# One pool for the eight PSUM banks, score halves placed alone, and two more transposes through the DMA crossbar, with new instruction lists

## The chip, the core and the metric

The kernel runs on one core of one Trainium2 chip. The metric is the device time of one execution in microseconds (us); the profile takes one execution apart by engine: PE (TensorE matmul) and PEld (its weight loads), ACT (ScalarE), DVE (VectorE), POOL (GpSimd) and SP (SyncE). POOL and SP issue nearly all DMAs here.

## What is computed

Two stages in a row, cut from the reference. The first is attention with ALiBi bias in a sliding window of 128, over 8 batches, 8 heads, 576 positions and head dimension 64:

```python
scores = scale * np.matmul(q, k.transpose(0, 1, 3, 2))
mask = (rel >= 0) & (rel < window)
scores = np.where(mask, scores + bias[None], -1000000000.0)
attn = np.exp(scores - max); attn = attn / (attn.sum + 1e-09)
x = np.matmul(attn, v)            # then (batch, seq, 8 * 64 = 512)
```

The second is an RWKV channel mix over x with the row before it (x_prev):

```python
xk = mu_k * x + (1 - mu_k) * x_prev
xr = mu_r * x + (1 - mu_r) * x_prev
k = np.maximum(xk @ w_k, 0.0)     # 512 -> 1024
v = k * k @ w_v                   # 1024 -> 512
out = 1 / (1 + np.exp(-(xr @ w_r))) * v
```

Inputs and output are fp32, and the matmuls run in bf16.

## The kernel before

**Attention.** A batch b is worked in four groups g of two heads. q and k come in position-major and are turned so that head dimension lies on the partitions: on PE for batches 0 to 3 (L1126, L1123, qk_quad at L1078, qk_some at L837), by DMA transposes from SP for batches 4 to 7 (flip, L535). The last 64 positions of a batch, its tail, are a load of their own; they are turned by PE for batches 0 to 3 (tails at L939, tails_full at L912) and by a DMA transpose for 4 to 7 (tail_flip, L628; the range XTT). `scores` (L726) multiplies q by k for two halves of the window, HALF0 and HALF1; each half fills two PSUM banks (one per head) and only HALF1 reads the tail. ACT takes the exponential (L740) and DVE multiplies by the mask with the bias in it (L753). `attend` (L781) multiplies by v, whose column of ones gives the row sum, into two PSUM banks; DVE takes the reciprocal (L787) and scales (L793) into xu. xu is turned back to feature-major xt: for batches 1 to 5 two groups at a time on PE (out_some, L837, with two copies on ACT, L696), for 6 and 7 by a DMA transpose from SP (out_flip, L902; the range XO). DVE makes the difference with the shifted rows (L880) and xk and xr (L887).

**Channel mix.** `channel_mix` works on pairs P of batches, in stretches of 256, 384 or 512 rows. For each of eight slices fo: four matmuls of x with w_k into one PSUM bank (L983), ReLU on ACT (L990), square on DVE or ACT (L964, L962). For each 128 rows: four matmuls with w_r into one bank (L1001) and tanh on ACT (L1008); eight matmuls with w_v into one bank, in two halves of four (L1017); DVE joins both into ot (L1022); SP stores it (L1047).

**Order.** Every operation is a `Node` of a `Plan`. `ORDER` at the top holds three lists of node numbers, written out by hand for PE, ACT and DVE: each of these engines runs its nodes in that order and no other. POOL and SP follow priorities, FAB stands for the DMA engines. `Plan.run` walks through planned times with costs per node, hands out buffers and PSUM banks (`Hold`, `take`, `pick`: the lowest free number), and emits instructions by planned start. Semaphore waits between engines are put in after that, from the order in which instructions that touch a tile were emitted. 90 small matmuls (L687) fill PE's gaps in the first 17 us.

**PSUM.** 2 KB per partition and bank, eight banks. They are split into `duo`, two tiles of two banks each (class p2: score halves and attend), and `uno`, four tiles of one bank each (class p1: everything else). A node that computes both halves of a score takes both duo tiles at once.

```python
duo = [pst.tile([128, 2, 512], FP32, name=f"duo{i}") for i in range(2)]
uno = [pst.tile([128, 512], FP32, name=f"uno{i}") for i in range(4)]
def one(h):
    return uno[h.idx if h.cls == "p1" else N1 + h.idx]
def two(h):
    return duo[h.idx]
```

`SS` names the batches whose two score halves are nodes of their own (none before), and `OH` those that use out_some.

Of the kernel before, what the change touches and what calls it, by code (L numbers as in the profile page):

```python
# [9 lines left out]
FP32 = mybir.dt.float32  # L10
# [28 lines left out]
""".split()],  # L39
    "ACT": [int(x) for x in """  # L40
# [11 lines left out]
""".split()],  # L52
    "DVE": [int(x) for x in """
# [187 lines left out]
def kernel(  # L241
# [14 lines left out]
    B, H, S, D = q.shape  # L256
# [10 lines left out]
    W = D + 1  # L267
# [5 lines left out]
    NQ, NA, NX, NV, NC = 4, 4, 4, 2, 2  # L273
    XB = range(4, B)
    XO = range(6, B)
# [22 lines left out]
    SS = ()  # L298
    OH = range(1, 6)
# [15 lines left out]
    XTT = range(4, B)  # L315
# [53 lines left out]
    duo = [pst.tile([128, 2, 512], FP32, name=f"duo{i}") for i in range(2)]  # L369
    uno = [pst.tile([128, 512], FP32, name=f"uno{i}") for i in range(4)]  # L370
    N1 = 4
    PT = "p1"

    def one(h):
        return uno[h.idx if h.cls == "p1" else N1 + h.idx]

    def two(h):
        return duo[h.idx]

    plan = Plan(dict(qx=2, p2=2, p1=N1, pt=4 - N1, qk=NQ, at=NA, xu=NX, vs=NV, cb=NC, ts=2, tt=2, xt=2, dl=2, dl0=4,  # L380
                     xk=2, rl=3, kk=3, rs=4, ot=NO),
                {}, WAIT)
# [14 lines left out]
    def op(e, dur, deps, prio, emit, need=(), free=()):  # L397
        return plan.add(e, dur, LAT.get(e, 0.2) if isinstance(e, str) else LAT[e[0]] if len(e) == 1 else 0.22,
                        deps, prio, emit, need, free)
# [274 lines left out]
    h_mu = Hold("p1")  # L674
# [9 lines left out]
    h_wm = Hold("p1")  # L684
# [13 lines left out]
    def scores(b, g, parts, bias, hq, ha, deps, prio, need, free):  # L698

        todo, dur = [], 0.0  # L700
        for (pieces, m0, tt) in parts:
            a0 = BASE[pieces[0][0]] + pieces[0][1] - 128 * pieces[0][0]
            w = sum(n for _, _, n in pieces)
            todo.append((pieces, m0, tt, a0, w, Hold("p2")))
            dur += sum(max(n / 2400 + .0025, .03) for _, _, n in pieces)
            dur += 0.01 + (2 * mm(w) if bias else 0)
# [24 lines left out]
        s = op(PE, (0.12 if bias else 0.02) + dur, deps, prio + (2,), emit, list(need) + [x[5] for x in todo], free)  # L731
# [27 lines left out]
    def attend(b, g, t0, t1, ha, deps, prio):  # L759
# [3 lines left out]
        hp, hx = Hold("p1" if 2 * nt * W <= 512 else "p2"), Hold("xu")  # L763
# [5 lines left out]
        def a5():  # L769
            if hp.cls == "p1":  # L770
                return one(hp)[:, 0:2 * nt * W].rearrange("p (h t c) -> p h t c", h=2, c=W)
            return two(hp)[:, :, 0:nt * W].rearrange("p h (t c) -> p h t c", c=W)
# [36 lines left out]
    def out_t(b, g, t0, t1, hx, deps, prio, hk, ht, late=None):  # L809
# [3 lines left out]
        hp = Hold(PT if b else "p1")  # L813
# [15 lines left out]
    def halves(n, block):  # L829

        hp = [Hold("p1"), Hold("p1")]

        def emit(e):
            for i in range(n):
                src, c = block(i)
                for r in range(2):
                    nc.tensor.transpose(  # L837
                        one(hp[r]).bitcast(BF16)[:, c:c + 64], src[64 * r:64 * r + 64],
                        ident[64 * r:64 * r + 64, 64 * r:64 * r + 64])

        return hp, emit
# [65 lines left out]
    def tails_full(b, prio, htt, hs):  # L907
        hp = Hold("p1")
# [16 lines left out]
    def tails(b, prio):  # L925
# [8 lines left out]
        hp = Hold("p1")  # L934
# [33 lines left out]
    def channel_mix(P, c0, c1, first, xks, xrs, order):  # L968
# [9 lines left out]
        for fo in range(NFO):  # L978
            hp, hr = Hold("p1"), Hold("rl")
# [16 lines left out]
        for i, c in enumerate(range(c0 // 128, c1 // 128)):  # L996
            hp, hs = Hold("p1"), Hold("rs")
# [12 lines left out]
            hv, ho = Hold("p1"), Hold("ot")  # L1010
# [16 lines left out]
            for a, b in ((0, FIN), (FIN, 512)) if final else ((0, 512),):  # L1027
                if a:
                    hv = Hold("p1")
# [40 lines left out]
    def qk_quad(b, g, nr, buf, deps, prio, c0, hq, take, free):  # L1070

        hp = [Hold("p1"), Hold("p1")]
# [25 lines left out]
    for part in range(2):  # L1098
# [3 lines left out]
        for g in range(G):  # L1102
# [13 lines left out]
            hp = Hold("p1") if part == 0 else None  # L1116
# [51 lines left out]
    def mask_pe(j):  # L1168
        hp = Hold("p2")
# [55 lines left out]
    def qk_full(b, g, prio):  # L1225
        hp, hq = Hold(PT), Hold("qk")
# [101 lines left out]
```

## Time and profile before

| what | value |
|---|---|
| time, median of 3 runs (lowest to highest) | 229.33 us (228.99 to 229.42) |
| the profiled execution: its time, its span | 228.84 us, 227.1 us |
| PE busy | 221.8 us, 98% of the span |
| DVE busy | 188.8 us, 83% |
| ACT busy | 155.0 us, 68% |
| POOL busy | 92.0 us, 41% |
| share of PE in the chain that ended last | 92% |

The span runs from the first to the last instruction that the profiler saw; the execution's own time is 1.7 us more. Busy time of PE counts each matmul with the time its result takes to come out, so neighbours overlap. The chain that ended last is followed back from the last instruction to what released it; the windows view gives busy time by stretch, the groups view the mean duration of one instruction of each kind.

### The profile page before, as it was taken

What the parts mean: (1) busy time and instruction counts of PE and PEld (TensorE: products, weight loads), DVE (VectorE), ACT (ScalarE), POOL (GpSimd) and SP (SyncE); (2) the same over time, 40 slices, a digit from 0 to 9 for tenths busy, and PEclk for the clock granted to TensorE, in tenths of its full rate; (3) what the DMA queues carried; (4) which work ended last, traced back from release to release, by engine and by line L of the source; (5) the groups of instructions that cost most, each with busy time, mean ns of one, the idle gap of its engine ahead of it and who ended that gap; (6) DMA issues with size and microseconds to landing.
All of it is one profiled execution on the core that took longest, in us unless ns stands there. A gap on an engine that the chain in (4) does not pass through costs nothing.

```text
span 227.1 us, 6442 instructions
## 1 busy us (share of the span) xinstructions
PE 221.8 (98%) x2587; PEld 133.2 (59%) x2587; DVE 188.8 (83%) x423; ACT 155.0 (68%) x279; POOL 92.0 (41%) x118
## 2 busy tenths in 40 slices
PE   8899999999999999999999999999999999999994
PEld 8576766755666755556666554546765455446552
DVE  6786999899879998899978996999899988963433
ACT  0678999999989984975868358768567564047511
POOL 8856726599962964385208750240000000000000
PEclk9999999999999999999999999999999999999999
DMA  6999999999999999999999999999150415430124
GB/s 165 179 185 200 197 196 175 199 180 151 196 156 165 137 130 180 168 182 147 211 180 158 120 185 231 177 136 222 30 135 3 123 46 52 131 136 3 49 92 139
DMA packets 129981, 33.19 MB, mean 146 GB/s; under 512 B 116632, under 2 KB 126112, under 8 KB 129952
## 3 DMA queue, kind: packets, MB, share of 16 engines
q0 software_dynamic: 95728, 16.26, 97.5%
q1 hardware_dynamic: 32480, 15.94, 34.1%
q10 hardware_dynamic: 1744, 0.59, 1.1%
q8 instruction: 20, 0.33, 0.6%
q14 instruction: 9, 0.07, 0.1%
HBM read 33.56 MB, written 9.44 MB: 189 GB/s over the span
## 4 chain that ended last, share of the span: by engine, by line
PE 92%; ACT 3%; DMA 2%; SPq 1%; issue 0%; DVE 0%; DVEq 0%; ACTq 0%
PE uno L983 28%; PE uno L1017 28%; PE uno L1001 13%; PE duo L726 7%; PE duo L781 7%; DMA qx<-in_q_dram 2%; PE uno L837 2%; PE uno L1078 2%; ACT at L740 1%; PE duo L713 1%; ACT qk L696 1%; PE uno L781 1%; SPq L550 1%; PE uno L687 1%; PE uno L820 1%; PE uno L939 0%
## 5 line engine op out<-in xcount | busy, mean ns | idle before, releaser
L983 PE MATMUL uno<-xk,wk_sb 128*128 128x256 bf16 (+2 forms) x416 | 72.0, 314 | 0.1
L740 ACT ACTIVATE at<-duo 128x1024 bf16<-128x1024 f32 (+2 forms) x68 | 65.5, 985 | 8.8 <-PE duo L726 8.5
L1017 PE MATMUL uno<-wv_sb,kk 128*128 128x512 bf16 (+2 forms) x296 | 69.7, 374 | 0.0
L990 ACT ACTIVATE rl<-uno 128x256 bf16<-128x256 f32 (+2 forms) x104 | 46.4, 471 | 26.4 <-PE uno L983 21.0
L983 PEld LDWEIGHTS <-wk_sb 128*128 128x128 bf16 x416 | 38.7, 98 | 24.2 <-issue 0.3
L1017 PEld LDWEIGHTS <-kk 128*128 128x128 bf16 x296 | 27.2, 98 | 27.3
L500 POOL DMA_DIRECT2D vs<-in_v_dram x32 | 28.4, 904 | 31.8 <-PE duo L781 25.9
L753 DVE TENSOR_TENSOR at<-at,mask 128x1024 bf16<-128x1024 bf16 x56 | 36.9, 682 | 1.8 <-ACT at L740 1.8
L964 DVE TENSOR_TENSOR kk<-rl 128x256 bf16<-128x256 bf16 (+2 forms) x94 | 30.2, 339 | 8.8 <-ACT rl L990 8.4
L1008 ACT ACTIVATE rs<-uno 128x512 bf16<-128x512 f32 x36 | 21.1, 604 | 22.2 <-PE uno L1001 22.1
L1001 PE MATMUL uno<-wr_sb,xr 128*128 128x512 bf16 x144 | 36.1, 379 | 0.0
L1022 DVE SCALAR_TENSOR_TENSOR ot<-rs,uno 128x512 f32<-128x512 bf16 (+2 forms) x37 | 24.4, 666 | 10.5 <-PE uno L1017 8.8
L887 DVE SCALAR_TENSOR_TENSOR xk<-dl,mu_sb,xt 128x576 bf16<-128x576 bf16 (+1 forms) x32 | 24.4, 779 | 0.0
L887 DVE SCALAR_TENSOR_TENSOR xr<-dl,mu_sb,xt 128x576 bf16<-128x576 bf16 (+1 forms) x32 | 24.3, 776 | 0.0
L781 PEld LDWEIGHTS <-at 128*128 128x128 bf16 x576 | 21.0, 97 | 4.7 <-ACT at L740 0.4
L793 DVE TENSOR_TENSOR xu<-duo,rc 128x640 bf16<-128x640 f32 x28 | 22.6, 815 | 0.2
L1001 PEld LDWEIGHTS <-xr 128*128 128x128 bf16 x144 | 13.3, 98 | 13.5 <-issue 0.2
L531 POOL DMA_DIRECT2D cb<-in_k_dram x20 | 17.5, 888 | 6.9 <-DMA vs<-in_v_dram 4.7
L781 PE MATMUL duo<-vs,at 128*128 128x65 bf16 x448 | 18.6, 193 | 0.0
L531 POOL DMA_DIRECT2D cb<-in_q_dram x20 | 17.7, 935 | 1.2 <-PE duo L781 1.1
L696 ACT COPY xt<-uno 128x640 bf16<-128x640 bf16 (+3 forms) x28 | 15.0, 583 | 3.3 <-PE uno L837 2.5
L880 DVE TENSOR_TENSOR dl<-xt 128x576 bf16<-128x576 bf16 (+1 forms) x32 | 13.5, 432 | 2.8 <-ACT xt L696 2.7
(83 smaller groups left out, 197.9 us busy)
## 6 DMA issues: line engine op xcount, KB each, us to landing
out_dram<-ot SPq DMA_DIRECT2D x30, 256.0 KB, 4.6
vs<-in_v_dram POOLq DMA_DIRECT2D x32, 128.0 KB, 7.8
cb<-in_q_dram POOLq DMA_DIRECT2D x20, 128.0 KB, 6.3
cb<-in_k_dram POOLq DMA_DIRECT2D x20, 128.0 KB, 12.1
out_dram<-ot SPq DMA_DIRECT2D x10, 128.0 KB, 1.8
wk_sb<-in_moe_w_k_dram POOLq DMA_DIRECT2D x2, 512.0 KB, 9.1
cb<-in_q_dram POOLq DMA_DIRECT2D x4, 256.0 KB, 9.7
cb<-in_k_dram POOLq DMA_DIRECT2D x4, 256.0 KB, 8.6
```

What stands on the lines that cost most here:

```text
L500: return dma(POOL, 256, issue_t(1024), lambda e: nc.gpsimd.dma_start(out=vs_buf[h.idx][:, j, :, 0:D], in_=v[b, :, 128 * j:128 * j + 128].r ...
L531: return [dma(POOL, 256, issue_t(1024), lambda e, r=r: nc.gpsimd.dma_start(out=cb_buf[h.idx][:, i, r], in_=src[:, :, r]), [g], kind="q") f ...
L740: lambda e, ah=ah, w=w, hp=hp: nc.scalar.activation(out=ah(), in_=two(hp)[:, :, 0:w], func=AF.Exp, scale=float(scale)), (), [hp])
L753: nc.vector.tensor_tensor(out=a, in0=a, in1=m, op=ALU.mult)
L781: nc.tensor.matmul(a[:, hl, t - t0], lhsT=at[:, lo:lo + 128], rhs=vs[:, u, 2 * g + hl, 0:W] if u < NF else tvb[:, 2 * g + hl, 0:W], start= ...
L887: lambda e: nc.vector.scalar_tensor_tensor(out=buf[hk.idx][:, g, e0 + c0:e0 + c1], in0=dls(), scalar=mu[:, g:g + 1], in1=xc(1), op0=ALU.mu ...
L964: nc.vector.tensor_tensor(out=out, in0=in_, in1=in_, op=ALU.mult)
L983: nc.tensor.matmul(one(hp)[:, 0:n], lhsT=wk_sb[:, po, 128 * fo:128 * fo + 128], rhs=xk_buf[hx.idx][:, po, c0:c1], start=(po == 0), stop=(p ...
L990: a = op(ACT, act_t(n), [s], pr, lambda e, hp=hp, hr=hr: nc.scalar.activation(out=rl_buf[hr.idx][:, 0:n], in_=one(hp)[:, 0:n], func=AF.Rel ...
L1001: nc.tensor.matmul(one(hp), lhsT=xr_buf[hx.idx][:, po, 128 * c:128 * c + 128], rhs=wr_sb[:, po], start=(po == 0), stop=(po == NPO - 1))
L1017: nc.tensor.matmul(one(hv)[:, a:b], lhsT=kk_buf[hk.idx][:, fo, o:o + 128], rhs=wv_sb[:, fo, a:b], start=(fo == 0), stop=(fo == NFO - 1))
L1022: nc.vector.scalar_tensor_tensor(out=ot_buf[ho.idx][:, a:b], in0=rs_buf[hs.idx][:, a:b], scalar=1.0, in1=one(hv)[:, a:b], op0=ALU.add, op1 ...
```

## The change

- `uno` goes; `duo` becomes four tiles of two banks. All PSUM holds are of one class, `p`, with eight places. A hold of one bank is half of a duo tile, a hold of two banks is a whole one. `pick` then takes its other branch: a single bank is taken beside a bank that is in use, if there is one, and a double one only where both banks of a tile are free.
- `SS` is range(1, B): for batches 1 to 7 each score half is a node of its own, with its own hold of two banks.
- `XO` begins at batch 5: its xu is turned by four DMA transposes from SP, and its two out_some groups with four ACT copies go.
- `XTT` begins at batch 3: its tail is turned by one DMA transpose, and one tails_full group of four transposes with a DVE copy goes.
- `n_split`, the number of output rows whose store is cut in two, follows from the count of DMAs: it falls from 5 to 0.
- The three lists of `ORDER` are new in full. Four squares of the channel mix stand on ACT instead of ten.

Line numbers of the changed kernel are lower by 2 from L687 on.

```diff
-    XO = range(6, B)
+    XO = range(5, B)
...
-    SS = ()
-    OH = range(1, 6)
+    SS = range(1, B)
+    OH = range(1, 5)
...
-    XTT = range(4, B)
+    XTT = range(3, B)
...
-    duo = [pst.tile([128, 2, 512], FP32, name=f"duo{i}") for i in range(2)]
-    uno = [pst.tile([128, 512], FP32, name=f"uno{i}") for i in range(4)]
-    N1 = 4
-    PT = "p1"
+    duo = [pst.tile([128, 2, 512], FP32, name=f"duo{i}") for i in range(4)]
 
     def one(h):
-        return uno[h.idx if h.cls == "p1" else N1 + h.idx]
+        return duo[h.idx // 2][:, h.idx % 2]
 
     def two(h):
-        return duo[h.idx]
-
-    plan = Plan(dict(qx=2, p2=2, p1=N1, pt=4 - N1, qk=NQ, at=NA, xu=NX, vs=NV, cb=NC, ts=2, tt=2, xt=2, dl=2, dl0=4,
+        return duo[h.idx // 2]
+
+    plan = Plan(dict(qx=2, p=8, qk=NQ, at=NA, xu=NX, vs=NV, cb=NC, ts=2, tt=2, xt=2, dl=2, dl0=4,
                      xk=2, rl=3, kk=3, rs=4, ot=NO),
-                {}, WAIT)
+                {"p": (0, 2, 4, 6)}, WAIT)
...
-            todo.append((pieces, m0, tt, a0, w, Hold("p2")))
+            todo.append((pieces, m0, tt, a0, w, Hold("p", 2)))
...
-        hp, hx = Hold("p1" if 2 * nt * W <= 512 else "p2"), Hold("xu")
+        hp, hx = Hold("p", 1 if 2 * nt * W <= 512 else 2), Hold("xu")
...
-            hp, hr = Hold("p1"), Hold("rl")
+            hp, hr = Hold("p"), Hold("rl")
```

The other holds change from "p1" and "p2" in the same way. The branch of `pick` that the pool now takes stood in the kernel already:

```python
if h.n == 2:
    for a in self.pairs[h.cls]:
        if a in free and a + 1 in free:
            return a
    return None
return max(free, key=lambda a: ((a ^ 1) not in free, a))
```

More of the change, by code (lines that the diff above doesn't have):

```diff
@@ L670 @@
         op0=ALU.mult), [n_ident], (0, 2 + h)) for h in range(H)]
-    h_mu = Hold("p1")
+    h_mu = Hold("p")
     def emit_mu(e):
@@ L682 @@
         out=mu_sb.rearrange("p i o -> p (i o)"), in_=one(h_mu)[:, 0:2 * NPO]), (), [h_mu])
-    h_wm = Hold("p1")
+    h_wm = Hold("p")
     def emit_warm(e):
@@ L730, in scores @@
             dur *= 1.6
-        s = op(PE, (0.12 if bias else 0.02) + dur, deps, prio + (2,), emit, list(need) + [x[5] for x in todo], free)
+        s = op(PE, (0.12 if bias else 0.01 * len(parts)) + dur, deps, prio + (2,), emit, list(need) + [x[5] for x in todo], free)
         s.rows = (128 if bias else 64, 64)
@@ L769, in a5 @@
         def a5():
-            if hp.cls == "p1":
+            if hp.n == 1:
                 return one(hp)[:, 0:2 * nt * W].rearrange("p (h t c) -> p h t c", h=2, c=W)
@@ L812, in out_t @@
         n = c1 - c0
-        hp = Hold(PT if b else "p1")
+        hp = Hold("p")
         def tp():
@@ L829, in halves @@
     def halves(n, block):
-        hp = [Hold("p1"), Hold("p1")]
+        hp = [Hold("p"), Hold("p")]
         def emit(e):
@@ L907, in tails_full @@
     def tails_full(b, prio, htt, hs):
-        hp = Hold("p1")
+        hp = Hold("p")
         def emit(e):
@@ L933, in tails @@
             return tails_full(b, prio, htt, hs)
-        hp = Hold("p1")
+        hp = Hold("p")
         def emit(e):
@@ L996, in channel_mix @@
         for i, c in enumerate(range(c0 // 128, c1 // 128)):
-            hp, hs = Hold("p1"), Hold("rs")
+            hp, hs = Hold("p"), Hold("rs")
             def emit3(e, c=c, hp=hp):
@@ L1009, in channel_mix @@
                 out=rs_buf[hs.idx], in_=one(hp), func=AF.Tanh, scale=0.5), [hs], [hp])
-            hv, ho = Hold("p1"), Hold("ot")
+            hv, ho = Hold("p"), Hold("ot")
             o = 128 * c - c0
@@ L1028, in channel_mix @@
                 if a:
-                    hv = Hold("p1")
+                    hv = Hold("p")
                 for half in range(2):
@@ L1070, in qk_quad @@
     def qk_quad(b, g, nr, buf, deps, prio, c0, hq, take, free):
-        hp = [Hold("p1"), Hold("p1")]
+        hp = [Hold("p"), Hold("p")]
         def emit(e):
@@ L1115 @@
                 cs = src1[g // 2]
-            hp = Hold("p1") if part == 0 else None
+            hp = Hold("p") if part == 0 else None
             def emit_t(e, part=part, g=g, hp=hp, f32=f32):
@@ L1168, in mask_pe @@
     def mask_pe(j):
-        hp = Hold("p2")
+        hp = Hold("p", 2)
         def emit(e):
@@ L1225, in qk_full @@
     def qk_full(b, g, prio):
-        hp, hq = Hold(PT), Hold("qk")
+        hp, hq = Hold("p"), Hold("qk")
         hc = ch[b]
```

85 rows, old and new, of the table ORDER are left out of this document.

## The prediction, made before the changed kernel ran

> **What bounds the kernel now.** I read the busy times first, then the windows, the waits, the chain that ended last, and last the groups by form, for prices. The page's first rows and one window over the middle of the run:
>
> ```profile
> span 227.1 us, 6442 instructions
> ...
> PE 221.8 (98%) x2587; PEld 133.2 (59%) x2587; DVE 188.8 (83%) x423; ACT 155.0 (68%) x279; POOL 92.0 (41%) x118
> ```
> ```profile
> 33.00:223.00 190.00, 189.97 (x2055) 110.38 (x2055) 162.03 (x328) 131.32 (x228) 69.91 (x84) 1.00 1.34 139
> ```
>
> From 33 to 223 us PE is busy 189.97 of 190.00 us. The granted clock is 1.00, so it doesn't enter. The two largest waits that have PE as the waiting engine lie in the first 8 us:
>
> ```profile
> PE uno L687 <- DVE warm L469: 1.0, 1, 1.0
> ...
> PE uno L1123 <- DMA qx<-in_q_dram: 0.5, 1, 0.5
> ```
>
> So the kernel is PE's work in a row, with about 33 us of start before it and a short end behind it. In this state nothing that another engine saves shows in the time, and two things do: work taken off PE, and a wait put onto it. Stretches of the chain give the prices of PE's work:
>
> ```profile
> 64.16 0.86 PE uno L1017 x4
> 65.03 0.22 PE uno L912 x4
> 65.25 0.55 PE duo L726 x12
> 65.80 0.29 PE uno L837 x20
> 66.09 1.83 PE uno L1017 x8
> ...
> 192.62 5.18 PE uno L1017 x24
> ...
> 198.67 1.73 PE uno L1017 x8
> ```
>
> A 512-column matmul takes 5.18/24 = 0.216 us of PE's row, and eight of them 1.73. Right behind L837, whose operands fill 64 of the 128 rows, eight take 1.83: going from 64-row work to full-row work costs 0.10, and so does going in (two score halves, 12 instructions, take 0.44 behind other 64-row work and 0.55 behind full-row work).
>
> **What goes off PE.** Two out_some groups of batch 5 at 0.29, and one tails_full group at 0.22: 0.80. Then the order. In the old list, 64-row nodes of batch 1 and later, with the quads of batch 0, stand in 39 runs between full-row work; in the new one in 36, though there are now 56 score halves in place of 28 pairs. The halves mostly stand two or three together, those of different groups side by side. Three runs less at two changes of 0.10 are 0.6. Sum: **-1.4 us**. Channel mix, attend and the scores keep their instructions.
>
> **What is put onto PE.** The two instruction lists, with the semaphore waits that each instruction carries, can be compared ahead of any run. I followed each wait of PE, ACT and DVE on one another to the instruction that ends it, and asked which PSUM bank each of the two touches. In the old kernel no wait joins two instructions that share a tile but no bank. In the new one **179** do (the warm-up matmuls apart): 63 of PE on ACT or DVE, 62 of ACT on PE, 20 of DVE on PE, 34 between ACT and DVE. A tile of two banks is thus guarded as one, and the pool's pick puts single banks beside a neighbour in use. The planned order knows only banks, so it doesn't provide for these waits.
>
> What one costs is a chain from PE over ACT or DVE to PE. An example stands behind 159 us of PE's work in the new list: a L1001 group fills one bank of a tile, the next L1017 group goes to the other bank, the tanh (L1008) that reads the first bank now waits for the L1017 group, and the L983 group next on PE goes into the tanh's bank and waits for it. Nothing of PE's lies between, so PE stands still for the whole chain. Rows for it:
>
> ```profile
> L1017 PE MATMUL uno<-wv_sb,kk 128*128 128x512 bf16 x280 | 67.8, 379 | 0.0
> ...
> L1022 DVE SCALAR_TENSOR_TENSOR ot<-rs,uno 128x512 f32<-128x512 bf16 x35 | 23.6, 680 | 9.6 <-PE uno L1017 7.9 <-DMA out_dram<-ot 0.8 <-ACT rs L1008 0.6
> ...
> L1008 ACT ACTIVATE rs<-uno 128x512 bf16<-128x512 f32 x36 | 21.1, 604 | 22.2 <-PE uno L1001 22.1
> ...
> L990 ACT ACTIVATE rl<-uno 128x256 bf16<-128x256 f32 x48 | 17.9, 392 | 9.3 <-PE uno L983 7.7 <-DVE kk L964 0.9 <-DVE ot L1022 0.4
> ...
> L990 ACT ACTIVATE rl<-uno 128x384 bf16<-128x384 f32 x32 | 15.3, 492 | 6.0 <-PE uno L983 4.4 <-DVE kk L964 1.4
> L990 ACT ACTIVATE rl<-uno 128x512 bf16<-128x512 f32 x24 | 14.0, 600 | 11.1 <-PE uno L983 8.8 <-issue 1.7 <-DVE kk L964 0.5
> ...
> L696 ACT COPY xt<-uno 128x640 bf16<-128x640 bf16 x10 | 7.1, 705 | 0.5 <-PE uno L837 0.4
> ```
> ```profile
> 9.23 0.72 ACT at L740
> 9.96 0.04 issue
> 10.00 0.49 PE duo L713 x2
> ```
>
> The matmul's result is there 0.379 - 0.216 = 0.16 us after its slot; ACT to PE takes 0.04, and I take the same from PE to ACT. A wait thus costs 0.20 + d + 0.04 - g, with d the duration on ACT or DVE and g the PE work that the list has between the group waited for and PE's waiting instruction. Taken through the list from 24 us of PE work on, and counting at each place only what the stalls before it haven't paid already, there are **33** with a price above zero:
>
> - 7 with g = 0: three at d = 0.60 (0.84 each), one at 0.49 (0.73), two at 0.39 (0.63), and the joining of the last output row, 0.55 on DVE (0.79). Sum 5.3.
> - 5 with g of 0.23 to 0.33, d 0.49 to 0.60: 0.50 to 0.52 each. Sum 2.6.
> - 10 with g of 0.43 to 0.55, d 0.39 to 0.71: 0.20 to 0.40 each. Sum 2.9.
> - 11 with g of 0.53 to 0.86: 0.06 to 0.10 each. Sum 0.9.
>
> Together **11.7 us**; three of the smallest have no neighbour's bank in them. The same count on the old list gives 4 places and 0.3 us, where the trace has none to speak of, so the method isn't biased high by much. It is the low end: it takes ACT and DVE to be free when their data are there. The high end takes each awaited ACT or DVE instruction to start only when PE has come to its place in the list: 24.3 us by the same rows (old list again 0.3). What lies between is ACT or DVE running late, and each stall of PE gives them time to catch up; both have some over the window above (131 and 162 of 190 us). I take the low end and a quarter of the rest: 11.7 + 3.1 = **14.8 us**. Behind a waiting PE instruction everything of PE's is queued, so nothing covers this.
>
> **Edits that I cost at nothing.** The start first, with the first transposes of q and k and the first L983 group:
>
> ```profile
> 5.08 0.39 PE L1126 MATMUL uno<-ident,qx 128*128 128x128 bf16 x4
> ```
> ```profile
> 17.52 1.31 PE uno L983 x12
> ```
>
> By the list, some 8.5 us of work lie before that group, so PE has been idle or in warm-up matmuls for 9 us by then, the first 5 of them for want of inputs. The new list puts other work there, and six priced waits on neighbour banks (1.1 us); ends -2 (list packs better) and +3 (ACT, which is 97% busy from 20 to 60 us, falls behind), taken as 0. The four transposes of batch 5 and the one of the tail go past SP's queue, at 1.2 us each to issue:
>
> ```profile
> xt<-xu SPq DMA_TRANSPOSE x8, 2.6
> tt<-ts SPq DMA_TRANSPOSE x4, 7.1
> ```
> ```profile
> qx<-cb SPq DMA_TRANSPOSE x32, 7.5
> ```
> ```profile
> L902 SPq DMA_TRANSPOSE xt<-xu x8: 1199/1207/1248, 162.7 to 192.8; - x8
> ```
> ```profile
> L793 DVE TENSOR_TENSOR xu<-duo,rc 128x640 bf16<-128x640 f32 x28 | 22.6, 815 | 0.2
> L887 DVE SCALAR_TENSOR_TENSOR xk<-dl,mu_sb,xt 128x576 bf16<-128x576 bf16 x28 | 22.3, 812 | 0.0
> ...
> L880 DVE TENSOR_TENSOR dl<-xt 128x576 bf16<-128x576 bf16 x28 | 12.3, 449 | 2.5 <-ACT xt L696 2.3
> ...
> L787 DVE RECIPROCAL rc<-duo 128x10 f32<-128x10 f32 x28 | 6.1, 217 | 4.3 <-PE duo L781 3.3 <-ACT qk L696 0.5
> ```
> ```profile
> 20.00:60.00 40.00, 39.85 (x713) 26.05 (x713) 37.42 (x82) 38.84 (x78) 28.78 (x36) 1.00 1.82 188
> ```
>
> The 2.6 is of a time with little other DMA, the 7.5 of the loaded stretch, where batch 5 falls. From the end of batch 5's last attend: 0.2 and 0.8 on DVE and as much as 0.2 to start, 1.2 of issue, 7.5, and 0.4 and 0.8 for difference and xk, 11.1 us; the new list has 17 us of PE work before the L983 group that needs it. The tail of batch 3 has a similar margin, because only the second score halves read it. If a landing were 5 us later than the median these covers would be gone, at up to 5 us. The four ACT copies and the DVE copy that go, and six squares from ACT to DVE, lie on engines that PE doesn't wait for now. The stores no longer cut in two are not the last three rows of blocks; nothing waits for them.
>
> **Sum.** The profiled execution took 228.84 us (span 227.1, and 1.7 around it): 228.84 - 1.4 + 14.8 = 242.2. It was 0.5 below the median of the runs shown, 229.33, so I name **242.5 us**.
>
> **Rivals.**
>
> 1. *The waits are all covered, and the time is that of PE's work:* 229.3 - 1.4 = 227.9 us, faster. For it: the planned times already keep two users of a bank apart, and with that alone the old list stalls for 0.3 us. Against it: in 7 places there is no PE work between the two ends of the chain. It decides at 0.9 us: only with all stalls together below that would the change be faster by more than 0.5 us. The Trainium skill, "PSUM — Partial Sum Buffer", section "PSUM bank collisions raise a hardware error", has it that engines may work on different banks at once and only the same bank needs a guard; if the program waited by that rule and no further, this would be the time. No row of the trace of before bears on it, since its one-bank tiles never put the question.
> 2. *The stalls come out smaller,* because some instruction on ACT starts earlier than I think: between 230 and 237 us. The low end of the count is 229.3 - 1.4 + 11.7 = 239.6; to come below 237 the chains must be a fifth shorter than my rows make them.
> 3. *ACT and DVE fall behind as well:* 62 ACT waits hold ACT for PE, in-order behind them exponentials that attend needs. High end: 229.3 - 1.4 + 24.3 + 3 = 255 us. For it: ACT 38.84 of 40 us between 20 and 60 us. Against it: the later stretches have room.
> 4. *The change doesn't do what it says:* the halves aren't alone in the list, and the pool only moves the same work: 229.3 us. It needs both terms to be nil.
> 5. *The crossbar is late,* at 5 us on top: 247 us.
>
> **Chances.** Forecast, between 237 and 251: 0.72. Rival 2: 0.07; rival 3, above 251: 0.08; rival 5, inside the range: 0.06; rival 1: 0.05; rival 4: 0.02. The range is 237 to 251, with 0.78 inside. A run of this kernel can be told from no change at about 0.2%, 0.5 us. Faster 0.05, same 0.02, slower 0.93.
>
> **What would show it.** Right: the waits view shows PE with rows of 0.5 us and more behind ACT L988, L1006, L694 and DVE L1020 (the new numbers of L990, L1008, L696, L1022), 10 us or more together; PE busy share falls to 91 to 94%; four fewer ACT copies; the number of L835 groups on xu falls by two. Wrong: PE busy still 98% (rival 1), PE waiting mainly for exponentials or xk (rivals 3 and 5), or the 12 us gathered in the first 33 us.

## The result, and the profile after

The changed kernel takes **260.96 us** (median of 4 runs, 260.26 to 262.11) against 229.16 us of the kernel before (228.96 to 229.42): 1.139 times as long, 95% interval 1.134 to 1.144, 31.8 us more. Slower was forecast, at 242.5 us with a range of 237 to 251; the time lies 10 us above the range.

First the page of the changed kernel, its span and busy times, and the window from 33 to 223 us that the prediction began with:

```profile
span 258.6 us, 6346 instructions
...
PE 228.9 (89%) x2543; PEld 133.7 (52%) x2543; DVE 190.1 (74%) x426; ACT 153.7 (59%) x271; POOL 92.2 (36%) x118
```
```profile
33.00:223.00 190.00, 169.76 (x1857) 96.58 (x1856) 150.47 (x306) 122.57 (x203) 70.10 (x85) 1.00 1.34 132
```

PE had 189.97 busy us of 190 there; now it has 169.76, at the same granted clock of 1.00. DVE and ACT have about as much work as before (190.1 and 153.7 us in all, 188.8 and 155.0 before) and have become idler too: all three wait for one another. In the waits view, PE as the waiting engine had two rows, 1.0 and 0.5 us, both at the start. Now it lists 49 stops of PE, 24.8 us in all; one of them, 0.5 us, is "issue", a stop without a wait, and is taken up at the end of the experiments. The longest rows, and the one for xk (us in total, times, longest):

```profile
PE duo L981 <- ACT rl L988: 2.7, 6, 0.6
PE duo L981 <- DVE ot L1020: 2.3, 5, 0.7
PE duo L1015 <- DVE ot L1020: 1.7, 3, 0.7
PE duo L981 <- ACT rs L1006: 1.5, 3, 0.7
PE duo L999 <- ACT rl L988: 1.5, 2, 1.0
PE duo L1015 <- ACT xt L694: 1.3, 1, 1.3
...
PE duo L981 <- DVE xk L885: 0.4, 1, 0.4
```

These are the releasers that the prediction named (relu, tanh, copies, joining of a row). The row for xk is small. The chain that ended last, by engine, says the same (PE had 92% of it before):

```profile
PE 68%; ACT 16%; DVE 11%; issue 4%; ACTq 0%; DVEq 0%
```

I also took the trace's PE starts one by one and subtracted the list's own pace (the prediction's rows). Over the stretch that the prediction counted, from 24 us of PE's work on, 50 stalls of more than 0.15 us sum to 30.0 us, spread over the whole stretch; the kernel before has none.

The DMA transposes that were added (the median us from issue to landing stands last):

```profile
xt<-xu SPq DMA_TRANSPOSE x12, 2.6
tt<-ts SPq DMA_TRANSPOSE x5, 7.8
```

They land about as fast as those before (2.6 and 7.1). The crossbar isn't late: PE waits once for xk, 0.4 us.

### The profile page after: what moved, and what is told of

It is laid out like the page before. It is cut to its first block, busy times and chain, and to the rows that moved or that the text cites. A ratio compares the mean times of both kernels' runs of the same rounds, so it can differ in the third digit from the quotient of the medians.

```text
span 258.6 us, 6346 instructions
## 1 busy us (share of the span) xinstructions
PE 228.9 (89%) x2543; PEld 133.7 (52%) x2543; DVE 190.1 (74%) x426; ACT 153.7 (59%) x271; POOL 92.2 (36%) x118
## 4 chain that ended last, share of the span: by engine, by line
PE 68%; ACT 16%; DVE 11%; issue 4%; ACTq 0%; DVEq 0%
PE duo L981 22%; PE duo L1015 21%; PE duo L999 11%; ACT rl L988 7%; DVE ot L1020 4%; PE duo L724 4%; PE duo L779 3%; PE duo L685 3%; ACT rs L1006 2%; ACT xt L694 2%; DVE at L751 2%; ACT qk L694 2%; PE duo L835 1%; ACT at L738 1%; DVE qk L694 1%
## 5 line engine op out<-in xcount | busy, mean ns | idle before, releaser
L981 PE MATMUL duo<-xk,wk_sb 128*128 128x256 bf16 (+2 forms) x416 | 71.4, 313 | 9.0 <-ACT rl L988 2.7
L1015 PE MATMUL duo<-wv_sb,kk 128*128 128x512 bf16 (+2 forms) x296 | 69.9, 373 | 5.2 <-DVE ot L1020 1.7
L988 ACT ACTIVATE rl<-duo 128x256 bf16<-128x256 f32 (+2 forms) x104 | 45.7, 469 | 45.4 <-PE duo L981 26.5
L738 ACT ACTIVATE at<-duo 128x1024 bf16<-128x1024 f32 (+2 forms) x68 | 63.7, 977 | 6.0 <-PE duo L724 5.7
L1015 PEld LDWEIGHTS <-kk 128*128 128x128 bf16 x296 | 27.4, 97 | 35.5 <-issue 8.0
L1006 ACT ACTIVATE rs<-duo 128x512 bf16<-128x512 f32 x36 | 20.8, 599 | 35.9 <-PE duo L999 20.5
L999 PE MATMUL duo<-wr_sb,xr 128*128 128x512 bf16 x144 | 36.3, 379 | 3.2 <-ACT rl L988 1.5
L1020 DVE SCALAR_TENSOR_TENSOR ot<-rs,duo 128x512 f32<-128x512 bf16 (+2 forms) x37 | 24.6, 670 | 15.6 <-PE duo L1015 4.5
L791 DVE TENSOR_TENSOR xu<-duo,rc 128x640 bf16<-128x640 f32 (+2 forms) x36 | 26.7, 745 | 2.0 <-PE duo L685 1.3
L779 PE MATMUL duo<-vs,at 128*128 128x65 bf16 x512 | 22.5, 193 | 1.0 <-ACT rs L1006 0.5
L785 DVE RECIPROCAL rc<-duo 128x10 f32<-128x10 f32 (+2 forms) x36 | 7.5, 210 | 14.1 <-PE duo L779 8.9
L878 DVE TENSOR_TENSOR dl<-xt 128x576 bf16<-128x576 bf16 (+1 forms) x32 | 13.3, 432 | 4.6 <-ACT xt L694 4.5
```

The source lines that it names most:

```text
L738: lambda e, ah=ah, w=w, hp=hp: nc.scalar.activation(out=ah(), in_=two(hp)[:, :, 0:w], func=AF.Exp, scale=float(scale)), (), [hp])
L779: nc.tensor.matmul(a[:, hl, t - t0], lhsT=at[:, lo:lo + 128], rhs=vs[:, u, 2 * g + hl, 0:W] if u < NF else tvb[:, 2 * g + hl, 0:W], start= ...
L981: nc.tensor.matmul(one(hp)[:, 0:n], lhsT=wk_sb[:, po, 128 * fo:128 * fo + 128], rhs=xk_buf[hx.idx][:, po, c0:c1], start=(po == 0), stop=(p ...
L988: a = op(ACT, act_t(n), [s], pr, lambda e, hp=hp, hr=hr: nc.scalar.activation(out=rl_buf[hr.idx][:, 0:n], in_=one(hp)[:, 0:n], func=AF.Rel ...
L999: nc.tensor.matmul(one(hp), lhsT=xr_buf[hx.idx][:, po, 128 * c:128 * c + 128], rhs=wr_sb[:, po], start=(po == 0), stop=(po == NPO - 1))
L1015: nc.tensor.matmul(one(hv)[:, a:b], lhsT=kk_buf[hk.idx][:, fo, o:o + 128], rhs=wv_sb[:, fo, a:b], start=(fo == 0), stop=(fo == NFO - 1))
```

## The experiments

Each kernel ran beside the kernel before on the same chip; "over before" is the difference of those medians.

### Take the neighbour-bank waits away

A neighbour-bank wait is one between two instructions that use different banks of one tile. The framework lets a program say that an instruction doesn't depend on another. A function at the end tells it so for each two instructions of different engines that use one bank each of the same tile, not the same bank, and share no other data.

```diff
+    by_bank(tc, list(nc.cur_bb.bb.instructions))
...
+                for (t2, b2, e), m in list(members.items()):
+                    if (t2, b2) != (t, 1 - b) or e == i.engine:
+                        continue
+                    keep = [j for j, jw, jr in m if sw & (jw | jr) or jw & sr]
+                    tc.declare_no_dep(i, group=f"{t}_{1 - b}_{e}", keep=keep, reason="other bank")
```

> The changed kernel with the same lists, banks and instructions; only the waits between two instructions that share a two-bank tile but no bank and no other data are taken away (179 on PE, ACT and DVE). Theory A, the tile guards cost nearly all of the 31.8 us: 227.9 us (229.3 less the 1.4 of work off PE), between 227 and 230, and PE busy 97 to 98% again. Theory B, the new order itself (halves alone, transposes through the crossbar, fewer squares on ACT) costs it: 245 us or more. Something between, 232 to 245, would mean that the guards are a part and the order another.

Measured: 229.50 us, before 229.42; ratio 1.0011, interval 0.9993 to 1.0029. Its page (29 of PE's 2543 matmul records are missing in this trace, so the 96% is a little low) and the window:

```profile
span 228.1 us, 6312 instructions
...
PE 219.5 (96%) x2514; PEld 132.4 (58%) x2543; DVE 188.4 (83%) x426; ACT 151.3 (66%) x271; POOL 92.2 (40%) x118
```
```profile
33.00:223.00 190.00, 186.44 (x1959) 108.03 (x1986) 162.63 (x331) 128.07 (x222) 70.00 (x84) 1.00 1.36 141
```

The whole loss is gone, with the same lists, banks and instructions. Theory A holds and theory B falls. By the rule of the Trainium skill, "PSUM — Partial Sum Buffer", section "PSUM bank collisions raise a hardware error", only the same bank needs a guard. This run agrees as far as it goes: a program that waits by that rule, and no further, takes 229.5 us here.

### Put only those waits into the old kernel

```diff
-    duo = [pst.tile([128, 2, 512], FP32, name=f"duo{i}") for i in range(2)]
-    uno = [pst.tile([128, 512], FP32, name=f"uno{i}") for i in range(4)]
+    duo = [pst.tile([128, 2, 512], FP32, name=f"duo{i}") for i in range(4)]
...
-        return uno[h.idx if h.cls == "p1" else N1 + h.idx]
+        return duo[2 + h.idx // 2][:, h.idx % 2]
```

> The kernel before with one edit: its four one-bank tiles become two two-bank tiles, each hold in the bank that it had. No list, no instruction and no bank changes; 224 waits on neighbour banks come in. Theory A: slower by 15 to 40 us, since the old list was planned without these waits as well: 245 to 270 us. Theory B: 229 to 232 us.

Measured: 274.18 us, 1.194 times the time before (1.191 to 1.197): 44.8 us, though no bank, list or instruction differs. That is 4 us above the upper end that theory A gave (270). Its page and its largest row of waits of PE (L982 and L989 are L983 and L990 of the kernel before):

```profile
PE 229.1 (84%) x2554; PEld 135.2 (50%) x2587; DVE 191.8 (71%) x423; ACT 157.4 (58%) x279; POOL 92.1 (34%) x118
```
```profile
PE duo L982 <- ACT rl L989: 8.0, 14, 0.9
```

This is the largest effect of the study, from turning four one-bank tiles into two of two banks. The old list suffers more than the new one.

### Which waits, and how they add up

Five kernels, three here and two below, differ from the first experiment in one condition each: which engines' neighbour-bank waits are left in.

```diff
-                    if (t2, b2) != (t, 1 - b) or e == i.engine:
+                    if (t2, b2) != (t, 1 - b) or e == i.engine or i.engine != mybir.EngineType.PE:
```

is the one without PE's own waits; the others have the condition turned accordingly.

> The changed kernel without PE's own waits on neighbour banks; ACT and DVE keep theirs, on PE and on each other (121 left). Theory A says that a stall is a chain out of PE over ACT or DVE and back to PE. If the way back is mostly one of the waits taken away, this gives 230 to 238 us. If ACT and DVE come late for their own sake, and PE's waits for its own bank then bite, 240 to 250 us. Theory B: over 255 us.

> The changed kernel without the waits of ACT and DVE on PE for a neighbour bank; PE's own waits on ACT and DVE stay, and those between ACT and DVE. Theory A: ACT and DVE are then on time, and what is left is 75 waits of PE, most of them on work that is long done: 230 to 240 us. If PE's own waits alone carry the loss: over 245 us. Theory B: over 255 us.

> The changed kernel without the neighbour-bank waits between ACT and DVE; those of PE on them and of them on PE stay (144 left, since some waits that lay behind the removed ones show themselves now). Of the 28 stalls of over 0.15 us that the changed kernel shows at places which the prediction had not priced, 10 run through such a wait, 6.9 us together. Theory C, chains of three links (PE to ACT to DVE to PE): 254 us, between 251 and 257. Theory D, mere queues on ACT and DVE: 259 us or more.

Measured: 246.77 without PE's own waits (17.4 over before), 241.84 without those of ACT and DVE on PE (12.4), 256.16 without those between ACT and DVE (26.6). Either half alone leaves much. The first came in its worse branch (240 to 250 us), the second between its two; only the third came as its theory had it, with chains over both ACT and DVE. The 50 stalls of the changed kernel, taken one by one, sort like this:

- At the **33 places that the prediction priced**, at 11.7 us together, the trace has 11.2 us (the three at 0.84 measured 0.84, 0.85 and 0.85).
- The other 18.8 us are at **28 places that it had not priced**. At 10 of them (6.9 us) the instruction that PE waits for has itself waited, for a neighbour's bank, on the other of ACT and DVE. At 12 (8.3 us) it waits for nothing at all: it stands behind another on ACT or DVE. Six have other reasons (3.6 us).

The chain of waits (start, us, what) shows the three sorts. The priced one is the example of the prediction, a tanh held for the neighbour's L1015 group; PE waits for it with nothing between:

```profile
195.58 0.88 PE duo L1015 x4
196.46 0.02 issue
196.48 0.61 ACT rs L1006
197.09 0.04 issue
197.13 0.60 PE duo L981 x4
```

Here ACT holds a copy of xt until the L1015 group in the neighbour's bank is through; PE waits for the copy behind it, which is held by nothing and must wait its turn. Two copies in a row, 1.19 us, where my count had no chain:

```profile
113.58 1.74 PE duo L1015 x8
115.32 0.02 issue
115.35 1.19 ACT xt L694 x2
116.54 0.04 issue
116.58 3.61 PE duo L1015 x16
```

And here the joining on DVE waits for a relu on ACT in the other bank of its tile, and PE for the joining:

```profile
87.63 0.02 issue
87.66 0.67 ACT rl L988 x2
88.32 0.02 issue
88.35 0.70 DVE ot L1020
89.05 0.04 issue
89.09 2.75 PE duo L1015 x12
```

So the price of a place was right and the count of places was not. Two more kernels test this, one with PE's own waits only, the other with those of ACT and DVE on PE only:

> The changed kernel with only PE's own waits on neighbour banks left (57 on ACT and DVE); no instruction of ACT or DVE is held for a neighbour bank. Theory Q: the price of a place was right, and what the count missed are instructions that stand behind a held one on ACT or DVE, or wait for it; with none held there, the count is complete: it gives 5.7 us here, 0.3 without neighbour waits, so 229.5 + 5.4 = 234.9 us (234 to 236.5). Theory R, each stall of PE costs more than its chain: at the 2.7 times of the changed kernel 244 us, and in any case over 239.

> The changed kernel with only the waits of ACT and DVE on PE left (83); PE waits for its own banks alone, and ACT and DVE don't hold one another for a neighbour. The count of chains over one instruction gives 9.3 us, so 238.5 us if it were complete. Theory Q: held instructions hold those behind them on ACT and DVE, so more: 241 to 247 us, not above the 246.8 of the kernel that also has the waits between ACT and DVE. Theory R: no difference from the count's ratio, 250 us or more.

Measured: 238.70 (9.8 over before, ratio 1.040 to 1.044) and 243.56 us (14.6). The second lies inside theory Q's range. The first is neither of the two cases that I wrote down: 3.8 us above Q's figure and 2.2 above its range, just below R's 239. Its trace says why. At the places counted, priced at 4.9 us, it has 5.7; so the stalls cost little more than their chains, far from 2.7 times, and R falls. But 4.0 us are at 11 places where the instruction that PE waits for stands behind others on ACT or DVE, or waits for one of those, in the plain order of work. Q was too narrow: an instruction ahead delays the awaited one whether it is held or merely runs.

With that, the same count can be carried through the order of each engine, each instruction of ACT and DVE starting behind the one ahead of it, at these paces (1.57 us for three, 1.54 for two):

```profile
196.48 1.57 ACT L1006 ACTIVATE rs<-duo 128x512 bf16<-128x512 f32 x3 [2.19 <-PE duo L1015]
```
```profile
113.00 1.54 DVE L885 SCALAR_TENSOR_TENSOR xr<-dl,mu_sb,xt 128x576 bf16<-128x576 bf16 x2
```

It is an estimate from rows and lists, made after these runs. Us over the same list without neighbour waits (the first line over the kernel before, the others over the first experiment):

| kernel | chains over one instruction | carried through each engine's order | measured |
|---|---|---|---|
| old list, paired tiles | 15.3 | 39.0 | 44.8 |
| changed kernel | 11.4 | 29.0 | 31.7 |
| without PE's own | 9.0 | 15.2 | 17.3 |
| without ACT's and DVE's on PE | 5.4 | 12.1 | 12.3 |
| without those between ACT and DVE | 12.2 | 25.2 | 26.5 |
| only PE's own | 5.4 | 10.2 | 9.7 |
| only those on PE | 9.0 | 13.3 | 14.5 |

### Other choices of a bank

```diff
-        return max(free, key=lambda a: ((a ^ 1) not in free, a))
+        return min(free)
```

> The changed kernel with another choice of a single bank: the lowest free one, in place of one beside a bank in use. The lists stay; 158 neighbour-bank waits in place of 179, and the prediction's count of two-link chains gives 9.1 us in place of 11.7. If the loss follows that count (31.5 to 11.7 in the changed kernel, 45 to 15.6 with the old list in paired tiles): 253 to 256 us. If it is the choice of bank that makes the loss: under 245 us. If the choice doesn't matter: 259 to 263 us.

Measured: 259.01 us, 29.5 over before, against 31.8 for the changed kernel. Two of its four runs had a mean granted clock of 0.985 and took 260.1 us; the two at 1.00 took 257.1 and 258.0, which lies between the branches written down. The ratio of the short count (9.1 to 11.7) isn't a measure of the loss: it would have given some 254. For the opposite rule, a single bank beside a free one, the long count was made before the run:

```diff
-        return max(free, key=lambda a: ((a ^ 1) not in free, a))
+        return max(free, key=lambda a: ((a ^ 1) in free, a))
```

> The changed kernel with single banks put, where possible, beside a free bank in place of one in use; 165 neighbour-bank waits. A count made before this run, with the prices of the prediction's rows but the chains carried through the order of ACT and of DVE (an instruction there waits for the ones ahead of it too, at the pace of three tanh in 1.57 us and two xk or xr in 1.54), gives 23.5 us over the kernel without neighbour waits; for the runs so far it gives 29.0 for the changed kernel (measured 31.5), 23.7 for the lowest bank first (29.5), 10.2 for PE's waits alone (9.2), 13.3 for those on PE alone (14.1). So 229.5 + 23.5 = 253.0 us, 251 to 259 with the misses so far. If placing banks apart were the cure: under 245 us.

Measured: 256.42 us, 27.6 over before; the count says 23.5, the range held. Over the first experiment the long count falls short in both of these kernels, with 23.7 against 29.4 us and 23.5 against 27.5: it finds most of the loss and not all, and what it misses wasn't traced. All three rules of choice leave 158 to 179 neighbour-bank waits and lose 27 to 32 us, so none of the three is a cure. A choice that leaves only few such waits was not tried.

### Where the 1.4 us went

Without neighbour waits the new list should have been 1.4 us faster than the old one, and takes the same time (0.1 us more, within the interval). In the trace of the first experiment PE stops twice in the middle of a group, where no instruction has a wait ("issue" is time in which the engine waited for nothing that the profile shows):

```profile
PE duo L835 <- issue: 1.3, 1, 1.3
...
PE duo L1076 <- issue: 0.4, 1, 0.4
```

Together 1.7 us. (Three more "issue" rows of this view, 0.2 us each, stand where a matmul's record is missing.) In the program's list of PE's instructions the stops stand before numbers 1722 and 954. The expectations below count the trace's PE records instead (matmuls and weight loads) and call them 1726 and 961; that count is off by a few. The stop of 0.5 us in the changed kernel itself stands before number 1722 too.

```diff
+    turns = iter(range(NWARM))
...
-        nc.tensor.matmul(one(h_wm)[:, 0:128], lhsT=warm, rhs=warm, start=True, stop=True)
+        if next(turns) % 3 != 2:
+            nc.tensor.matmul(one(h_wm)[:, 0:128], lhsT=warm, rhs=warm, start=True, stop=True)
```

> The changed kernel without all neighbour-bank waits, and with 60 warm-up matmuls in place of 90, so that each later PE instruction stands 60 places earlier in PE's instruction stream (a matmul and its weight load each). In the kernel without these waits PE stops for 1.3 us in the middle of an L835 group, where no instruction waits for anything. If that is the loading of PE's instructions, the stop moves to another place or goes: 228.0 to 229.0 us. If it hangs on the work at that place, it stays in the same L835 group: 229.3 to 229.8 us. If the warm-up is missed, the granted clock in the first 20 us falls and the time rises.

Measured: 231.99 us (ratio 1.007 to 1.012). The time is outside what was expected, and the trace shows two reasons. The granted clock between 20 and 60 us is 0.96, the third number from the end of this row; it is 1.00 in the kernel before:

```profile
20.00:60.00 40.00, 35.63 (x655) 23.71 (x658) 32.24 (x74) 34.90 (x70) 29.43 (x37) 0.96 1.90 183
```

In finer stretches all of the drop lies from 32 to 36 us, at 0.57; up to 32 us and from 36 to 60 us the clock is 1.00. The other reason stands just before it: the stops got longer (lines are 3 higher in this kernel), and the longest ends at 31.0 us, about 1 us before the clock falls:

```profile
PE duo L1079 <- issue: 2.0, 1, 2.0
PE duo L838 <- issue: 1.5, 1, 1.5
```

So the drop of the clock isn't the one that the expectation named: in the first 20 us it is 1.00. Nor is it shown that the missing warm-up matmuls bring it about: the kernel with the lowest bank first has all 90, and after three stalls of 0.4 to 0.8 us from 28.7 us on its clock is 0.53 from 32 to 36 and 0.50 from 36 to 39 us.

The stops stand before instructions 954 and 1466 of PE's list, and a third of 0.5 us before 1721, though all of the work has moved 60 places. 1466 - 954 is 2 x 256, and 1722 - 954 is 3 x 256 (the trace's records, a few of which are missing or not of this kind, gave the 255 of the next expectations). The page of the first experiment lists 20 packets of instructions, 0.33 MB together, some 16 KB each; its list has 5096 PE instructions, 255 for a packet (with 60 warm-up matmuls the list is 60 instructions shorter, and its page has 19 packets):

```profile
q8 instruction: 20, 0.33, 0.6%
```

So the stops belong to places in PE's instruction stream, whole blocks of 256 apart, in a stretch of short matmuls. Two kernels then shift the stream by 10 records either way (95 and 85 warm-up matmuls).

> The changed kernel without the neighbour-bank waits, and with 95 warm-up matmuls in place of 90: each later PE instruction stands 10 records (a matmul and its weight load each) further back in PE's stream. With 90 PE stops without a wait at its records 961 and 1726 (0.4 and 1.3 us), with 60 at 961, 1471 and 1726: distances of 255 and 3 x 255. Theory F, PE's instructions come in blocks of 255 records and PE stops when it is through one in less than about 4 us: the shortest blocks were 3.0 and 3.6 us long with 90; with 95 the same work falls into blocks of 4.4 us and more, no stop is left, and the time is 229.5 - 1.7 = 227.8 us (227.4 to 228.3), faster than the kernel before. Theory G, the stops hang on the work at those places: 229.3 to 229.8 us.

> The same with 85 warm-up matmuls, 10 records the other way. Theory F: the two shortest blocks are 3.9 us, the stops 0.1 to 0.4 us each, at records 961 and 1471: 228.0 to 228.6 us. Theory G: 229.3 to 229.8 us, with the 1.3 us still in the same L835 group.

Measured: 229.60 (ratio 1.0020 to 1.0074) and 229.66 us (1.0011 to 1.0043), both above what theory F gave. By the times alone theory G would stand (229.3 to 229.8 us); the places speak against it: with 95 the stop at 954 is all but gone (0.1 us) and 0.5 us is left at 1722, with 85 there are 1.0 us at 954 and 0.4 at 1722, while G wanted the same stops at the same work. So F has the places right and G is out, but F's bound of about 4 us for a block fails. A block that it put at 4.4 us or more still ended in a stop of 0.5 us; so did one of 5.1 us in the changed kernel and one of 5.6 us with 60 warm-up matmuls, while blocks of 3.9 to 4.2 us ran through without one.

The profiled execution with 95 took 228.83 us, 1.1 less than that of the first experiment, as its shorter stops would have it, but over all runs nothing is gained; what the stops cost in the executions that weren't profiled isn't known. No version here beats the kernel before. That PE's loading of instructions makes the stops is an inference from the spacing and the packets; what sets their length stays open.

## Why the prediction was right and wrong, step by step

- **What bounds the kernel, and that a wait on PE shows in full:** right. Stalls and time agree (30.0 us of stalls from 24 us of work on, 31.5 us of span).
- **The mechanism, a two-bank tile guarded as one:** right, and shown both ways: without these waits 229.5 us, with them alone in the old kernel 274.2.
- **"Together 11.7 us ... It is the low end", and "a quarter of the rest":** this is the step that failed. The term taken as 14.8 us measured 31.7. The prices were right at their places (11.7 priced, 11.2 measured), but a chain was only counted when the one instruction that PE waits for was itself held by PE. Chains over two engines, and over an instruction ahead on the same engine, were left to the quarter. Nor was 24.3 a high end: it let the awaited instruction start when PE had come to its place in the list, and one behind a held instruction starts later. That the short count gave 0.3 us for the old list was no test, since in that list nothing holds ACT or DVE for PE's sake without need.
- **The start, taken as 0 between -2 and +3:** 2.5 us lost (at 24 us of PE's work the trace is 12.3 us behind the list, 9.8 before); inside its ends.
- **-1.4 us of PE work:** the instructions went as counted (160 transposes of xu on L835 in place of 200), but the first experiment shows nothing of it within 0.3%. In its profiled execution two stops without a wait take 1.7 us, which the prediction had not foreseen; that they are what ate the 1.4 us in every run is likely and not shown.
- **Edits costed at nothing:** right as far as the runs show (transposes of xu land in 2.6 us as before, PE waits for xk once, 0.4 us, and the first experiment, which has all of these edits, takes 229.5 us).
- **Rivals:** the first (all covered) is refuted, and its 227.9 us isn't reached even without the waits. The second, the fourth and the fifth are out. The third, ACT and DVE fall behind as well, is nearest to what happened, with 0.08 and 255 us. It named exponentials behind held instructions; the traces have copies, tanh, relu and joinings there, and PE's matmuls wait for an exponential in one row only, 0.2 us (its weight loads for 0.5 us):

```profile
PE duo L724 <- ACT at L738: 0.2, 1, 0.2
```

- **What would show it:** the named releasers are there; PE's share fell to 89%, below the 91 to 94% named.

## What to carry to other kernels

A tile is a unit of waiting. Put two banks into one tile only if one instruction needs both, or tell the framework which pairs don't depend on one another; with a hand-written order the difference was 31 to 45 us of 229. When a new wait is priced on an in-order machine, follow the chain through everything that stands ahead of the awaited instruction on its engine, not only through the data: in the changed kernel the price of a single link was right to 5%, the loss 2.7 times the sum of the links.

## What the hardware showed unexpectedly

PE stopped for 0.4 to 2.0 us without any wait, at fixed places of its instruction stream (whole multiples of 256 instructions apart), behind blocks of short matmuls that ran through in 2.8 to 5.6 us; blocks of 3.9 to 4.2 us also passed without a stop. And the granted clock fell to about half for 3.4 us, 1 us after a stop of 2.0 us, in a kernel whose clock was 1.00 up to then; in another it did so for 7 us after three shorter stalls.
